# A block-sparse attention followed by a Fourier mix and an MLP: the planner that orders its instructions tries some hundred orders with shifted priorities

## The chip, the core and the metric

The kernel runs on one core of a Trainium2 chip. The metric is the device time of one execution in microseconds. Before the change the median of three executions is 297.0 us (296.93 to 297.16). One further execution was profiled; it took 297.32 us, of which the profile's span covers 295.1 us.

## The reference, cut to what matters

There are 4 batches of 8 heads, 768 positions and a head width of 64. For every query the mean key of each of 12 blocks of 64 keys is scored, the three best blocks and the query's own block are kept, and an ordinary causal softmax attention runs over the kept keys. Its output, laid out as `x` with 512 columns per position, is mixed by a two-dimensional Fourier transform and goes through an MLP:

```python
scores = np.where(mask & causal, scale * q @ k.T, -1e9)
x = softmax(scores) @ v                                  # per head, then heads side by side
mixed = np.real(np.fft.fft(np.fft.fft(x, axis=1), axis=2))
u = x + mixed
un = (u - mean(u)) / sqrt(var(u) + 1e-6)
out = u + np.maximum(un @ w_ch1, 0.0) @ w_ch2            # 512 -> 2048 -> 512
```

## The kernel before

**The work.** Two heads make a pair, and there are 16 pairs, four to a batch. `attention(p)` (line 455) loads q, k and v of a pair, casts them to 16 bits, turns k and q with TensorE (`k_turn` 496, `q_turn` 552; from the eighth pair on q is turned by a DMA on SP's queue), forms the block means (`k_sums` 509, `spread` 532), scores the blocks (`gates` 563), picks the best three (lines 588 to 626), turns the choice into a mask (`m_turn` 631, `spell` 638), and then runs, for each head, six chunks of scores (`scores` 657, matmuls on lines 661 and 666), each followed by an exponential on ScalarE (line 677), and one product with the values (`attend` 692, 21 matmuls on line 695) whose result VectorE divides by the row sums (lines 704 and 707). `fourier(b)` (718) needs the four pairs of its batch: VectorE or GpSimd forms sums and differences (lines 727 to 748), TensorE does the first transform (`stage1` 762, matmuls on lines 766 and 770) and the second (`stage2` 793, matmuls on line 800), VectorE adds x (806), takes statistics (813, 816), ScalarE makes the reciprocal deviation (824, 828), VectorE forms the bias (832), and `apply` (838, matmul input written on line 840 or 844) normalises. The first half of batch 0 is then turned by TensorE (`un_turn` 862, matmuls on line 864), everything else by a DMA on SP's queue (line 856). `mlp(b)` (956) runs 32 groups of four 384-column matmuls up (line 968), a clipping copy on ScalarE or VectorE (980, 982), and 24 groups of four 512-column matmuls down (line 997); the last batch's downward product is done with seven smaller products per block (`down_seven` 919, line 942).

**What sets the order.** None of this is issued as it is written. Every step is recorded by `Plan.op` (106) as an operation with a rank, the engines that could run it with a cost in us for each, the keys that it reads and writes, the PSUM banks that it uses, and for some a release time `rel`, before which the plan does not start it. `Plan.schedule` (139) then simulates five engines: again and again it takes, over all engines, the operation that could start first, with the lower rank going first between equals, and gives it to the engine on which it would end first. What comes out is one order for each engine's queue, and for operations that two engines could run, the engine. Only that order reaches the chip: each engine runs its list in order and waits on semaphores for its inputs, and neither the planned times nor the release times are kept there. Release times are given to the loads and casts of pairs 7 and later (`release`, 259: 70 us for pair 7, then 15.5 us a pair) and to the weights' DMAs on GpSimd's queue (`weight`, 390; first use in lines 1022 and 1026). The plan adds 0.5 us to what TensorE waits for from other engines after 70 us of plan time, and 2.5 us to what a DMA brings after the first 8 us.

**Fillers.** One thing of the plan other than the order does reach the chip. Until 75 us of plan time, where TensorE would sit idle for over 0.25 us ahead of an operation, the plan puts `int(idle / 0.2 + 1)` matmuls of 512 columns on a tile of zeros ahead of it (`filler`, 408, line 410); they write a spare bank that nothing reads. Eleven more stand at the very start. They are ordinary instructions in TensorE's queue: once issued they take their time whether or not the wait is there.

**Tiles in the profile.** `loads`, `turned`, `keys` and `vals` hold the attention's inputs, `x` its output, `fs` and `pm` the Fourier sums, `ty` and `tr` the half-transformed data, `u` the sum to be normalised, `unT` the turned normalised rows, `hT` the hidden layer, `w` the weights, `bank` any PSUM bank, `warm` the zeros of the fillers.

Of the kernel before, what the change touches and what calls it, by code (L numbers as in the profile page):

```python
# [2 lines left out]

# [78 lines left out]
class Plan:  # L83
# [22 lines left out]
    def op(self, rank, engs, fn, r=(), w=(), ps=(), dma=0.0, port=False, pre=(), after=(), rel=0.0,  # L106
# [29 lines left out]
        self.ops.append(o)  # L136
        return o

    def schedule(self):
        ops = self.ops  # L140
        free = dict(PE=1.0, ACT=1.5, DVE=0.9, POOL=1.3, SP=0.75)
        ready = {e: [] for e in free}
        for o in ops:
            o.wait = len(o.deps)
            o.ready = o.rel
            for d in o.deps:
                ops[d].users.append(o.i)
        cand = {e: set() for e in free}

        def offer(o):  # L150
            for e in o.engs:
                cand[e].add(o.i)

        for o in ops:
            if o.wait == 0:
                offer(o)
        banks = sorted((self.FILL_TO if b == self.SPARE else 0.0, b) for b in range(8))
        used = dict.fromkeys(self.CAPS, 0)
        releases = []
        dma_free = dict(POOL=0.0, SP=0.0)  # L160
        landing = {e: [] for e in free}
        port_free, holder = 0.0, None
        order = []
        left = len(ops)

        def begin(o, e, t):
            if o.port and e in ("DVE", "POOL"):
                t = max(t, port_free + (self.LAT["DVE"] if e == "POOL" and holder else 0.0))
            return max(t, free[e])

        while left:
            best = None
            for e, c in cand.items():
                now = free[e]
                pick = None
                for i in c:
                    o = ops[i]
                    t = o.ready
                    new = [p for p in o.ps if p.bank is None]
                    if new:  # L180
                        if len(banks) < len(new) or any(
                                used[p.kind] + len(new) > self.CAPS[p.kind] for p in new):
                            continue
                        t = max(t, banks[len(new) - 1][0])
                    if (o.dma or o.turn) and e != "POOL" and len(landing[e]) >= self.DEPTH:
                        t = max(t, landing[e][-self.DEPTH])
                    st = begin(o, e, t)
                    if len(o.engs) > 1:
                        end = st + o.engs[e]
                        if any(begin(o, x, t) + y < end - 1e-9 for x, y in o.engs.items() if x != e):  # L190
                            continue
                    key = (st, o.rank, i)
                    if pick is None or key < pick[0]:
                        pick = (key, o)
                if pick and (best is None or pick[0][0] < best[0][0]):
                    best = (pick[0], e, pick[1])

            if releases and (best is None or releases[0][0] <= best[0][0]):
                t, b, kind = heapq.heappop(releases)
                used[kind] -= 1  # L200
                banks.append((t, b))
                banks.sort()
                continue
            assert best is not None, "no work can start"
            (st, _, _), e, o = best
            for c in cand.values():
                c.discard(o.i)
            for p in o.ps:
                if p.bank is None:
                    p.bank = banks.pop(0)[1]  # L210
                    used[p.kind] += 1
            if e == "PE" and st < self.FILL_TO:
                o.fill = int((st - free[e]) / 0.2 + 1.0) if st - free[e] > 0.25 else 0
            o.eng, o.start = e, st
            free[e] = st + o.engs[e]
            if o.port and e in ("DVE", "POOL"):
                port_free = free[e]
                if e == "POOL":
                    o.hold, holder = holder, None
                elif st < self.HOLD_TO:  # L220
                    holder = o
            o.done = free[e] + self.LAT[e]
            if o.dma:
                mine, other = ("POOL", "SP") if e == "POOL" else ("SP", "POOL")
                go = max(dma_free[mine], free[e])
                shared = max(0.0, dma_free[other] - go)
                dma_free[mine] = go + (2 * o.dma if 2 * o.dma <= shared else o.dma + shared / 2)
                o.done = dma_free[mine] + (2.6 if e == "POOL" else 1.9)
                landing[e].append(o.done)
            if o.turn:  # L230
                o.done = free[e] + 1.2
                landing[e].append(o.done)
            order.append(o)
            left -= 1
            for p in o.ps:
                p.left -= 1
                if p.left == 0:
                    heapq.heappush(releases, (o.done, p.bank, p.kind))
            for u in o.users:
                v = ops[u]  # L240
                v.wait -= 1
                at = o.done
                if e in v.engs and len(v.engs) == 1 and not o.dma and not o.turn:
                    at = free[e] + self.OWN[e]
                elif o.dma or o.turn:
                    at += self.LANDING if st > 8.0 else 0.0
                elif "PE" in v.engs and o.done > self.SLACK_FROM:
                    at += self.SLACK
                v.ready = max(v.ready, at)
                if v.wait == 0:  # L250
                    offer(v)
        order.sort(key=lambda o: (o.start, o.i))
        return order
# [3 lines left out]


def release(p):
    return 0.0 if p < 7 else 70.0 + 15.5 * (p - 7)  # L260

# [20 lines left out]
def kernel(  # L284
# [10 lines left out]
    B, H, _, D = q.shape  # L295
# [87 lines left out]
    P = Plan()  # L383
# [19 lines left out]
    for i in range(2):  # L403
        small(0.2 + i, "DVE", 0.06,
              lambda x, n, i=i: nc.vector.memset(ind32[64 * i:64 * i + 64, i:i + 1], 1.0),
              r=["ind32"], w=["ind32"])

    def filler(n):
        for _ in range(n):
            nc.tensor.matmul(bank32[P.SPARE], warm[:, 0:128], warm, start=True, stop=True)  # L410
# [18 lines left out]
    def load(p, rank, what, e, q_="SP"):  # L429
        b, hp = divmod(p, HP)  # L430
        i = slot(p)
        t, dst, src = dict(k=("kn", kn[i][:, :, e, :], k), q=("qn", qn[i][:, e], q),
                           v=("vn", vn[i][:, e], v))[what]
        dma(rank, q_, dst, src[b, 2 * hp + e].rearrange("(st p) d -> p st d", p=128),
            [(t, i, e)], 0.72 if p < 3 else 0.85, rel=0.0 if p < 7 else max(60.0, release(p) - 18.0))
# [598 lines left out]

    made = {}
    with tc.manual_schedule():
        for o in P.schedule():
            filler(o.fill)
            made[o.i] = o.fn(o.eng, o)
            if o.hold is not None:  # L1040
                tc.add_manual_dep(made[o.i].ins, made[o.hold.i].ins.name, mybir.DependencyInfo(
                    mybir.DependencyClass.Sync, mybir.DependencyReason.DATA), reason="port")
# [30 lines left out]
```

## Time and profile before

| what | before |
|---|---|
| median of three executions | 297.0 us |
| the profiled execution | 297.32 us |
| its span | 295.1 us |
| TensorE (PE) busy, share of the span | 98% |
| VectorE (DVE) busy | 72% |
| ScalarE (ACT) busy | 61% |
| GpSimd (POOL) busy | 42% |
| filler matmuls on line 410 | 67 of 3011 matmuls |

PE is TensorE's matmuls and PEld its weight loads, which run beside them. The ends of matmuls are modelled in the profile and reach into the next matmul, so the time that a row of matmuls really took is read from the chain of waits, which gives start and length of consecutive pieces, and not from their mean duration. In the view by windows each engine's entry is its busy time in the stretch in us, with the number of instructions in brackets, then the granted TensorE clock, the DMA share and GB/s. In the timeline a row gives start, length, engine, line, operation, tiles and count, and in square brackets the idle time of that engine before the row, with what ended it.

### The profile page before, as it was taken

The page shows a single profiled execution, that of the slowest core. Times are in us where ns is not written, and L with a number is a line of the kernel's source. Part 1 is how long each engine was busy: PE and PEld are TensorE (multiplying, and loading weights), DVE is VectorE, ACT ScalarE, POOL GpSimd, SP SyncE. Part 2 cuts the span into 40 slices and gives each one's busy share as a digit, 9 for nine tenths or more (in the row PEclk, how much of TensorE's full clock was granted, in tenths as well). Part 3 has the DMA queues.
Part 4 walks back from the last instruction along what each step waited for, and adds up shares of the span by engine and source line. Part 5 has one row for each costly group of instructions (what it writes and reads, how often), then busy time and mean ns, then how long its engine had stood idle before and what let it go on. Part 6 is the DMA issues. An engine that isn't in the chain of part 4 may idle for free.

```text
span 295.1 us, 8026 instructions
## 1 busy us (share of the span) xinstructions
PE 289.9 (98%) x3011; PEld 196.6 (67%) x3011; DVE 213.8 (72%) x716; ACT 180.9 (61%) x398; POOL 125.1 (42%) x248
## 2 busy tenths in 40 slices
PE   8999999999999999999999999999999999999995
PEld 3778786866646677567656686566655764566884
DVE  4899999897735689967564979937936694047885
ACT  3479988877804787367808687288743863477100
POOL 5558787564729155646656185456111000000000
PEclk9999999999999999999999999999999999999999
DMA  8999999998349706498824837733001005200132
GB/s 206 259 238 231 214 286 206 198 216 146 71 101 258 165 0 136 114 211 186 191 61 90 198 56 170 153 75 89 3 36 38 37 2 125 89 2 0 35 109 71
DMA packets 108773, 37.41 MB, mean 127 GB/s; under 512 B 101192, under 2 KB 104948, under 8 KB 108736
## 3 DMA queue, kind: packets, MB, share of 16 engines
q1 hardware_dynamic: 104272, 32.06, 47.4%
q0 software_dynamic: 3536, 4.56, 8.8%
q8 instruction: 23, 0.38, 0.5%
q10 hardware_dynamic: 928, 0.30, 0.4%
q14 instruction: 14, 0.11, 0.1%
HBM read 28.52 MB, written 6.29 MB: 118 GB/s over the span
## 4 chain that ended last, share of the span: by engine, by line
PE 95%; DVE 1%; ACT 1%; POOL 1%; issue 1%; ACTq 0%; POOLq 0%
PE bank L968 28%; PE bank L997 21%; PE bank L666 12%; PE bank L695 6%; PE bank L942 6%; PE bank L410 6%; PE bank L800 3%; PE bank L766 3%; PE bank L498 2%; PE bank L517 1%; PE bank L554 1%; PE bank L661 1%; PE bank L633 1%; ACT turned L677 1%; PE bank L569 1%; PE bank L770 1%
## 5 line engine op out<-in xcount | busy, mean ns | idle before, releaser
L677 ACT ACTIVATE turned<-bank 128x512 f16<-128x512 f32 x192 | 89.0, 583 | 22.4 <-PE bank L666 21.6
L968 PE MATMUL bank<-unT,w 128*128 128x384 f16 x512 | 90.3, 326 | 0.0
L980 ACT ACTIVATE hT<-bank 128x384 f16<-128x384 f32 x111 | 54.6, 498 | 28.4 <-PE bank L968 27.3
L968 PEld LDWEIGHTS <-w 128*128 128x128 f16 x512 | 48.3, 98 | 29.9
L997 PE MATMUL bank<-w,hT 128*128 128x512 f16 x288 | 67.4, 379 | 0.0
L666 PE MATMUL bank<-turned,keys 76*128 76x128 f16 (+3 forms) x384 | 50.1, 259 | 0.0
L997 PEld LDWEIGHTS <-hT 128*128 128x128 f16 x288 | 26.6, 97 | 27.3
L666 PEld LDWEIGHTS <-keys 76*128 76x128 f16 x384 | 29.4, 97 | 11.5 <-issue 0.2
L683 POOL TENSOR_SCALAR_AFFINE_SELECT turned<-turned 128x512 f16<-128x512 f16 (+1 forms) x44 | 22.2, 523 | 30.5 <-ACT turned L677 24.7
L695 PEld LDWEIGHTS <-turned 128*128 128x128 f16 x672 | 24.1, 97 | 4.6 <-ACT turned L677 0.7
L486 POOL TENSOR_TENSOR loads<-loads 128x384 f16<-128x384 f32 x25 | 22.9, 917 | 7.4 <-DVE fs L727 2.8
L695 PE MATMUL bank<-vals,turned 128*128 128x65 f16 x672 | 25.5, 193 | 0.1
L643 DVE TENSOR_SCALAR turned<-bank 12x384 f16<-12x384 f16 x64 | 20.6, 321 | 6.0 <-issue 2.7
L715 POOL CAST loads<-loads 128x384 f16<-128x384 f32 x24 | 12.2, 508 | 22.9 <-DVE pm L738 5.9
L481 POOL TENSOR_TENSOR turned<-loads,turned 128x320 f16<-128x320 f32 x26 | 20.7, 795 | 1.0 <-DVE fs L727 0.7
L410 PE MATMUL bank<-warm 128*128 128x512 f16 x67 | 19.7, 428 | 1.3 <-DVE warm L398 1.3
L704 DVE RECIPROCAL rcp<-bank 128x6 f32<-128x6 f32 x32 | 6.0, 189 | 19.1 <-PE bank L695 16.9
L1003 DVE TENSOR_TENSOR u<-bank,u 128x512 f32<-128x512 f32 x18 | 12.4, 687 | 8.7 <-PE bank L997 7.2
L707 DVE TENSOR_TENSOR x<-bank,rcp 128x384 f16<-128x384 f32 x32 | 17.7, 554 | 0.7
L714 ACT COPY keys<-bank 64x768 f16<-64x768 f16 x11 | 8.8, 797 | 14.9 <-PE bank L498 13.2
L806 DVE TENSOR_TENSOR u<-bank,x 128x512 f32<-128x512 f32 x24 | 15.4, 678 | 1.2 <-PE bank L800 1.2
L813 DVE BATCH_NORM_STATS2 bst<-u 128x6 f32<-128x512 f32 x24 | 15.6, 670 | 0.0
(112 smaller groups left out, 409.5 us busy)
## 6 DMA issues: line engine op xcount, KB each, us to landing
loads<-in_k_dram SPq DMA_DIRECT2D x28, 192.0 KB, 3.5
loads<-in_v_dram SPq DMA_DIRECT2D x28, 192.0 KB, 3.7
loads<-in_q_dram SPq DMA_DIRECT2D x26, 192.0 KB, 3.4
out_dram<-u SPq DMA_DIRECT2D x18, 256.0 KB, 2.3
w<-in_moe_w_ch_dram POOLq DMA_DIRECT2D x16, 256.0 KB, 7.2
out_dram<-u SPq DMA_DIRECT2D x12, 128.0 KB, 1.7
hT<-in_k_dram SPq DMA_DIRECT2D x4, 192.0 KB, 3.8
hT<-in_q_dram SPq DMA_DIRECT2D x4, 192.0 KB, 3.8
```

The costliest lines, as they stand in the source:

```text
L410: nc.tensor.matmul(bank32[P.SPARE], warm[:, 0:128], warm, start=True, stop=True)
L481: lambda x, n, hi=hi, lo=lo, e=e: eng[x].tensor_tensor(out=lo, in0=qn[a][:, e, 1:NST], in1=hi[:, 1:NST], op=OP.subtract),
L486: lambda x, n, kh=kh, kl=kl, e=e: eng[x].tensor_tensor(out=kl, in0=kn[a][:, :, e, :], in1=kh, op=OP.subtract),
L643: nc.vector.tensor_scalar(out=rows[:, i::2, :], in0=turned[at:at + NB, 0:3 - i, :], scalar1=-NEG, scalar2=NEG, op0=OP.mult, op1=OP.add)
L666: nc.tensor.matmul(bank32[sp.bank][:, co:co + a1 - a0], KI[e][g3][0:76, 128 * jt:128 * jt + 128], QG[e][g3][0:76, a0:a1], start=not added, ...
L677: lambda x, n, sp=sp, pt=pt, at=at, wid=wid: nc.scalar.activation(out=pt[:, at:at + wid], in_=bank32[sp.bank][:, 0:wid], func=AF.Exp, scal ...
L683: lambda x, n, pt=pt, at=at, nd=nd: nc.gpsimd.affine_select(out=pt[:, at:at + 128 * nd].rearrange("p (a c) -> p a c", a=nd), in_=pt[:, at: ...
L695: nc.tensor.matmul(o[:, st, 0:65], pt[:, col:col + 128], V16[v4][:, e, jt, 0:65], start=(i == 0), stop=(i == 20))
L942: nc.tensor.matmul(bank32[mp.bank][:, 0:256], A[i][:, z, :], Bm[i][:, z, :], start=(z == 0), stop=(z == 7))
L968: nc.tensor.matmul(bank32[hp_.bank][:, 0:384], w1[:, dt, 128 * it:128 * it + 128], unT[:, dt, 384 * hf:384 * hf + 384], start=(dt == 0), s ...
L980: nc.scalar.activation(out=o, in_=i_, func=AF.Relu)
L997: nc.tensor.matmul(bank32[cp.bank], hT[hf][:, it, 128 * j:128 * j + 128], w2[:, it, :], start=(it == 0), stop=(it == NIT - 1))
```

## The change

The plan is no longer made once. `Plan.search` makes it, then 600 times moves something at random, makes the plan again, and keeps the move if the planned end is no later. What it moves are the release times over 59 us (one of them and all later ones together, or one to three of them apart) and the ranks between 0 and 30000 (all ranks in a stretch of 8, 100 or 500 together, or one, two or four of them apart). The random numbers start from a fixed seed, so that the same order comes out on every build. The starting point differs in one number as well: the release of pairs 8 and later is spaced by 15.0 us and not by 15.5. `Plan.schedule` itself is rewritten to be quicker; it picks by the same rule. No operation, cost, tile or instruction of the computation is added or taken away. The number of fillers is part of what a plan decides.

```diff
+    def search(self, rounds, seed):
+        rng = random.Random(seed)
+        groups = {}
+        for o in self.ops:
+            if 0 < o.rank < 30000:
+                groups.setdefault(("rank", o.rank), []).append(o)
+            if o.rel > 59.0:
+                groups.setdefault(("rel", o.rel), []).append(o)
...
+        last = max(o.done for o in self.schedule())
+        for _ in range(rounds):
+            what = rng.random()
+            if what < 0.15:
+                at, by = rng.choice(rels), rng.gauss(0, rng.choice([0.5, 2, 5]))
+                moved = [(g, by) for g in rels if g >= at]
...
+            elif what < 0.75:
+                at, wide = rng.choice(ranks)[1], rng.choice([8, 100, 500])
+                by = rng.gauss(0, rng.choice([20, 200, 800]))
+                moved = [(g, by) for g in ranks if at <= g[1] < at + wide]
...
+            self.reset()
+            try:
+                end = max(o.done for o in self.schedule())
+            except AssertionError:
+                end = last + 1.0
+            if end <= last + 1e-9:
+                last = end
+            else:
+                for o, rank, rel in old:
+                    o.rank, o.rel = rank, rel
+        self.reset()
+        return self.schedule()
...
 def release(p):
-    return 0.0 if p < 7 else 70.0 + 15.5 * (p - 7)
+    return 0.0 if p < 7 else 70.0 + 15.0 * (p - 7)
...
-        for o in P.schedule():
+        for o in P.search(600, 7):
             filler(o.fill)
             made[o.i] = o.fn(o.eng, o)
```

More of the change, by code (lines that the diff above doesn't have):

```diff
@@ L2 @@
 import heapq
+import random
 from contextlib import ExitStack
@@ L137, in op, with reset @@
         return o
+    def reset(self):
+        for o in self.ops:
+            o.users = []
+            o.eng = o.start = o.done = o.hold = None
+            o.fill = 0
+            for p in o.ps:
+                p.left, p.bank = 0, None
+        for o in self.ops:
+            for p in o.ps:
+                p.left += 1
+    def search(self, rounds, seed):
+        rng = random.Random(seed)
+        groups = {}
+        for o in self.ops:
+            if 0 < o.rank < 30000:
+                groups.setdefault(("rank", o.rank), []).append(o)
+            if o.rel > 59.0:
+                groups.setdefault(("rel", o.rel), []).append(o)
+        rels = sorted(g for g in groups if g[0] == "rel")
+        ranks = sorted(g for g in groups if g[0] == "rank")
+        last = max(o.done for o in self.schedule())
[4 more added lines that the diff above has]
+                moved = [(g, by) for g in rels if g >= at]
+            elif what < 0.3:
+                moved = [(g, rng.gauss(0, rng.choice([0.3, 1, 3])))
+                         for g in rng.sample(rels, rng.choice([1, 2, 3]))]
+            elif what < 0.75:
[3 more added lines that the diff above has]
+            else:
+                moved = [(g, rng.gauss(0, rng.choice([5, 50, 500])))
+                         for g in rng.sample(ranks, rng.choice([1, 2, 4]))]
+            old = [(o, o.rank, o.rel) for g, _ in moved for o in groups[g]]
+            for (name, _), by in moved:
+                for o in groups[(name, _)]:
+                    setattr(o, name, getattr(o, name) + by)
+            self.reset()
[5 more added lines that the diff above has]
+                last = end
+            else:
+                for o, rank, rel in old:
+                    o.rank, o.rel = rank, rel
+        self.reset()
+        return self.schedule()
     def schedule(self):
@@ L172, in schedule @@
             best = None
-            for e, c in cand.items():
-                now = free[e]
+            for e in sorted(free, key=free.get):
+                c, now = cand[e], free[e]
+                if best is not None and now > best[0][0]:
+                    break
                 pick = None
+                limit = best[0][0] if best is not None else 1e9
                 for i in c:
@@ L178, in schedule @@
                     t = o.ready
-                    new = [p for p in o.ps if p.bank is None]
+                    if (t if t > now else now) > limit:
+                        continue
+                    new = [p for p in o.ps if p.bank is None] if o.ps else None
                     if new:
@@ L186, in schedule @@
                         t = max(t, landing[e][-self.DEPTH])
-                    st = begin(o, e, t)
+                    st = begin(o, e, t) if o.port else (t if t > now else now)
+                    key = (st, o.rank, i)
+                    if st > limit or pick is not None and key > pick[0]:
+                        continue
                     if len(o.engs) > 1:
[L189 to L194, printed above, removed]
+                        end = st + o.engs[e] - 1e-9
+                        for x, y in o.engs.items():
+                            if x != e and begin(o, x, t) + y < end:
+                                break
+                        else:
+                            pick, limit = (key, o), st
+                        continue
+                    pick, limit = (key, o), st
                 if pick and (best is None or pick[0][0] < best[0][0]):
```

## The prediction

> **What bounds the kernel now.** I read the page first, for which engine the time belongs to.
>
> ```profile
> span 295.1 us, 8026 instructions
> ...
> PE 289.9 (98%) x3011; PEld 196.6 (67%) x3011; DVE 213.8 (72%) x716; ACT 180.9 (61%) x398; POOL 125.1 (42%) x248
> ...
> DMA  8999999998349706498824837733001005200132
> ```
>
> TensorE is busy nearly throughout, but a busy matmul row need not be useful work. So I cut the span at three points of the chain of waits: 62.94, where the last big group of fillers begins; 66.63, where the first MLP matmul (L968) starts; and 273.62, where the last product (L942) starts.
>
> ```profile
> 0.00:62.94 62.94, 60.90 (x896) 45.85 (x897) 54.52 (x219) 47.77 (x106) 43.07 (x75) 1.00 1.08 229
> 62.94:66.63 3.69, 3.69 (x28) 2.04 (x27) 3.51 (x19) 2.10 (x3) 1.73 (x6) 1.00 1.23 205
> 66.63:273.62 206.99, 206.99 (x1924) 132.46 (x1923) 140.14 (x435) 130.54 (x288) 80.26 (x169) 1.00 0.44 100
> 273.62:292.00 18.38, 18.34 (x169) 16.20 (x166) 15.18 (x45) 0.49 (x1) 0.00 (x0) 1.00 0.22 72
> ```
>
> From 66.63 to 292.0 TensorE has no gap (the second number of a row is its busy time). The same view for the fillers' line alone (L410) shows where they stand, and the chain of waits gives the pace of equal matmuls at different places (start, length, count):
>
> ```profile
> 0.00:66.60 66.60, 19.63 (x67) 6.32 (x67) 1.00 1.09 228
> 66.60:295.10 228.50, 0.03 (x1) 0.00 (x0) 1.00 0.42 97
> ```
>
> ```profile
> 1.27 5.73 PE bank L410 x13
> ...
> 12.24 1.32 PE bank L410 x6
> ...
> 62.94 1.94 PE bank L410 x9
> ...
> 65.55 1.08 PE bank L410 x5
> ...
> 100.67 5.86 PE bank L968 x36
> ...
> 148.20 5.19 PE bank L997 x24
> ...
> 242.46 10.36 PE bank L997 x48
> 252.82 20.80 PE bank L968 x128
> ```
>
> L968 runs at 5.86/36 = 163 ns a matmul at 100 us, amid attention, and at 20.80/128 = 163 ns at 253 us, where nothing else is left; L997 at 216 ns at both places. So nothing is hidden under modelled ends: after 66.6 us TensorE does a fixed amount of useful work at its own pace, and the planner cannot shorten that, only break it. What it can shorten is the head. There, all 67 fillers stand. Thirteen take 5.73 us at the start, at 441 ns each; the other 54 run at 1.94/9 = 216 ns, and 54 x 0.216 = 11.7 us. Beside them the head holds little visible idle time: 62.94 - 60.90 = 2.04 us, of which 1.27 us is before the first filler. TensorE's own waits say the same:
>
> ```profile
> PE bank L410 <- DVE warm L398: 1.3, 1, 1.3
> PE bank L498 <- ACT turned L714: 0.4, 1, 0.4
> PE bank L534 <- DVE ka L527: 0.2, 1, 0.2
> ```
>
> So the kernel is bound by TensorE's queue, fillers included, and its only movable part is some 12 us of fillers ahead of 66.6 us.
>
> **The change part by part.** The instruction orders of the two built programs tell what the search did. TensorE has the same useful matmuls in both, and the same ones ahead of the first L968 group; its last 72 operations stand in the same order, and so do SP's last 14 DMAs, so the end after TensorE (292 to 295.1) stays. Line 410 has 58 matmuls instead of 67. Counted by place: the 13 at the start, 4, 2 and 2 more before 18 us, 3 near 33 us and the 5 just ahead of the first L968 group stay. Between 12 and 15 us, 6 + 3 + 3 become 5 + 3 + 2. Near 36 us, 5 become 4. Between 47 and 61 us, 3 + 4 + 2 + 3 become 6 + 2 + 3, in other places. Ahead of the first `un_turn` (L864), 9 become 4.
>
> *The nine fillers.* At 0.216 us each: two at 12 to 15 us, 0.43; one at 36 us, 0.22; one net at 47 to 61 us, 0.22; five ahead of L864, 1.08. Sum 1.94 us.
>
> *Is the wait behind them gone as well?* A filler taken out where its wait stays gives nothing, so I look at the largest place, which is the chain that leads to the MLP.
>
> ```profile
> 57.35 1.31 PE bank L800 x12
> ...
> 64.88 0.67 PE bank L864 x12
> ```
>
> ```profile
> 57.82 1.89 DVE L806 TENSOR_TENSOR u<-bank,x 128x512 f32<-128x512 f32 x3
> ...
> 62.53 0.68 DVE L806 TENSOR_TENSOR u<-bank,x 128x512 f32<-128x512 f32 x1
> 63.13 0.15 DVE L832 SCALAR_TENSOR_TENSOR nmr<-stat,rstd 128x3 f32<-128x3 f32 x1
> ...
> 64.00 0.53 DVE L844 TENSOR_SCALAR x<-u,stat,rstd 128x512 f16<-128x512 f32 x1
> ```
>
> ```profile
> 58.98 0.60 ACT L677 ACTIVATE turned<-bank 128x512 f16<-128x512 f32 x1 [0.76 <-PE bank L666]
> 59.84 2.23 ACT L677 ACTIVATE turned<-bank 128x512 f16<-128x512 f32 x5 [0.26 <-PE bank L666]
> 61.92 0.33 ACT L824 ACTIVATE lnv<-stat,eps 128x3 f32<-128x3 f32 x1
> ...
> 63.31 1.52 ACT L840 ACTIVATE x<-u,nmr,rstd 128x512 f16<-128x512 f32 x2 [0.82 <-DVE nmr L832]
> ```
>
> The first normalised tile leaves ACT near 63.31 + 0.76 = 64.07 (two in 1.52 us), and the third tile at 63.31 + 1.52 = 64.83; L864 follows at 64.88, the end of the nine fillers. So of the 1.08 us up to 0.8 is filler that overshoots the first tile. The rest needs the chain itself to be earlier. In the changed order it is. Between the last two `stage1` groups and the first L800 stood six chunks of scores, `spread` and three fillers; now four chunks stand there and no filler (3 x 0.216 = 0.65 us for the fillers alone), so L806 starts earlier. And the L666 chunks for which ACT idled 0.76 + 0.26 = 1.02 us ahead of L677 stand closer together, ahead of both products with the values, so L824, behind twelve exponentials in both orders, comes about 1 us earlier. What is late next is `unT`'s copy, under the five fillers that stay.
>
> *Waits that come back.* At the three smaller places (0.43 + 0.22 + 0.22 = 0.86 us) no row says whether the wait goes too. The bounds: all comes back, which leaves 1.08; or none does and the 0.77 us of visible idle time after the first filler goes as well, which makes 2.7. The fillers overshoot there too (a planned idle time is rounded up to whole fillers), so I stay close to the plan and take 0.15 us back.
>
> *Everything after 66.6 us.* Ranks and release times moved nearly everywhere, and 69 operations change engine (33 copies on L714/L715, 23 clipping copies, 8 normalisations, 4 Fourier sums, one difference). As long as every input is there in time this is worth 0: cover is TensorE's own queue, without a gap over 206.99 us. If the cover goes, each late input costs its lateness in full; that is rival B. Release times matter only as order: SP's loads of pairs 7 to 15 now stand in other places between the DMA transposes. The busy DMA share after 66.63 is 0.44, so transfers have room.
>
> *Sum.* 297.32 - 1.94 + 0.15 = 295.5 us on the profiled execution (span 293.3). That execution stands 0.32 us above the median of 297.0, so the median comes out at **295.2 us**.
>
> **The rivals.**
>
> A. *The waits take the fillers' place.* If the chain through DVE and ACT sets the first L968, the nine fillers are replaced by idle time: 297.0, give or take 0.3. For it: DVE is busy 54.52 of the first 62.94 us and 3.51 of the next 3.69. Against: L864 started when the fillers ended, and only 0.77 us of idle time is visible in front of 62.94.
>
> B. *ScalarE becomes the bound near 200 us; slower.* In the changed order the last product with the values stands ahead of 24 L997 groups and 51 L968 groups, before ahead of 14 and 48. That is 10 x 4 x 0.216 + 3 x 4 x 0.163 = 10.6 us earlier, so the exponentials of the last pairs have to be done that much sooner.
>
> ```profile
> 190.00:200.00 10.00, 10.00 (x114) 6.46 (x112) 5.17 (x22) 7.02 (x15) 5.40 (x15) 1.00 0.42 107
> 200.00:205.00 5.00, 5.00 (x50) 3.36 (x48) 2.95 (x9) 4.24 (x10) 3.74 (x6) 1.00 0.35 83
> 205.00:210.00 5.00, 5.00 (x62) 3.45 (x61) 4.94 (x12) 5.00 (x13) 0.64 (x1) 1.00 0.04 8
> ```
>
> ```profile
> L677 ACT ACTIVATE turned<-bank 128x512 f16<-128x512 f32 x192 | 89.0, 583 | 22.4 <-PE bank L666 21.6
> ```
>
> ACT (the fourth engine entry) has 2.98 + 0.76 + 0 = 3.7 us free there, six exponentials of 0.583 us. It decides from the seventh that has to be pulled forward: twelve, one pair's, would be 7.0 - 3.7 = 3.3 us late, and the time 295.2 + 3.3 = 298.5. Against: TensorE can place MLP groups between, and ACT's whole load from 66.63 to 273.62 is 130.54 of 206.99.
>
> C. *TensorE's clock falls.* The first 13 fillers took 441 ns each, later ones 216, while the granted clock reads 1.00 in both windows; so the array starts slow in a way that this column does not show, and fillers end that. If one of the thinned places let it fall again, the price is that of the start: 13 x (0.441 - 0.216) = 2.9 us, so 298.1. Against: the longest wait of TensorE after the start is 0.4 us, and the planner still fills every planned wait over 0.25 us in the head. The Trainium skill (TensorE: Matmul & The Clock Gate, "What's actually happening") has the rule for it: half rate after about 3.4 us of an idle window, full rate after as long a busy one. The start of this trace took longer, 5.73 us of busy fillers before the first fast row; no row here shows the fall.
>
> D. *More than fillers goes*: the other bound above, 297.0 - 2.7 = 294.3.
>
> That the search kept nothing is excluded by the orders: nine fillers are gone.
>
> **How the numbers follow.** Forecast 0.72 (295.2, between 294.6 and 296.1), D 0.10, A 0.08, B 0.07, C 0.03. Faster by over 0.2% (below 296.4, about what a measurement of this kernel can tell from no change) are the forecast and D, 0.82; the same is A, 0.08; slower are B and C, 0.10. The range goes from D's time to A's, 294.3 to 297.0; outside lie B, C and half of A and D, 0.19.
>
> **What would show it.** Right: 58 matmuls on L410; the first L968 near 64.8 instead of 66.63; from there to the end of L942 the same 225.4 us; ACT's two idle times ahead of L677 near 59 gone. Wrong: TensorE idle rows ahead of L864 or L800 (A); pieces of ACT L677 in the chain after 190 us, or busy TensorE time below the window's length there (B); L666 or L864 matmuls at twice their pace in the head (C). A first L968 as early as forecast with a time that is not would put the fault after 66.6 us.

## The result and the profile after

The changed kernel takes 295.74 us (median of five executions, 295.36 to 295.79) against 297.0 us for the kernel before in the same measurement (296.89 to 297.16): ratio 0.9952, 95% interval 0.9941 to 0.9962. So it is about 1.3 us faster, where 1.8 us were forecast. The profiled execution took 295.36 us, which is the fastest of the five, 0.38 us under their median; the profiled execution before stood 0.32 us above its own. So the two traces differ by more (1.96 us) than the medians do. In the changed kernel's file the lines of the code stand 66 further down: fillers are L476, the matmuls up L1034, the last product L1008, `un_turn` L930, `stage2` L866, the attention's scores L732, and the copies out of PSUM L780 (ScalarE) and L781 (VectorE).

The page of the changed kernel:

```profile
span 293.6 us, 8001 instructions
...
PE 287.7 (98%) x3002; PEld 194.6 (66%) x3002; DVE 210.5 (72%) x704; ACT 185.0 (63%) x407; POOL 129.2 (44%) x251
...
L476 PE MATMUL bank<-warm 128*128 128x512 f16 x58 | 16.3, 412 | 1.3 <-DVE warm L464 1.3
```

58 fillers, as the orders said. Now the span is split as before, at the start of the last fillers, of the first matmul up and of the last product, in the view by windows (length, then busy time of PE, PEld, DVE, ACT, POOL, granted clock, DMA share, GB/s), and the pieces of the chain of waits that give these points (start, length, count):

```profile
0.00:61.32 61.32, 59.27 (x892) 44.71 (x893) 53.82 (x217) 49.35 (x109) 43.51 (x74) 1.00 1.07 225
61.32:63.95 2.63, 2.63 (x23) 1.55 (x22) 2.63 (x8) 2.17 (x4) 0.81 (x1) 1.00 1.19 200
63.95:271.90 207.95, 207.42 (x1924) 132.15 (x1923) 138.35 (x436) 133.03 (x294) 84.90 (x177) 1.00 0.50 103
271.90:290.25 18.35, 18.35 (x169) 16.20 (x166) 15.26 (x45) 0.49 (x1) 0.00 (x0) 1.00 0.22 72
```

```profile
61.32 0.88 PE bank L476 x4
62.20 0.67 PE bank L930 x12
62.87 1.08 PE bank L476 x5
63.95 4.55 PE bank L1034 x28
...
251.11 20.80 PE bank L1034 x128
271.91 18.35 PE bank L1008 x168
```

The head, which is all that stands ahead of the first matmul up, ends 2.68 us earlier (63.95 instead of 66.63), more than the nine fillers. But the stretch behind it, with the same 1924 matmuls, is 207.95 us long and not 206.99: 0.96 us of the gain is given back. TensorE is no longer busy throughout there, and all its visible idle time lies in one place. The row of the four us from 106, first for the kernel before and then for the changed one:

```profile
106.00:110.00 4.00, 4.00 (x47) 3.57 (x45) 2.59 (x7) 3.22 (x7) 3.06 (x9) 1.00 0.00 0
```

```profile
106.00:110.00 4.00, 3.47 (x31) 2.24 (x29) 2.34 (x6) 3.34 (x9) 0.05 (x1) 1.00 0.03 6
```

0.53 us of visible idle time is the whole difference of 207.95 and 207.42. More hides under modelled ends, as the timeline of TensorE there shows (start, length, engine, line, tiles, count, in brackets the idle time before):

```profile
107.17 0.38 PE L732 MATMUL bank<-turned,keys 76*128 76x128 f16 x4 [0.18 <-DVE tr L781]
107.39 0.20 PE L600 MATMUL bank<-ka,sm 128*128 128x24 f16 x2
107.45 0.81 PE L1034 MATMUL bank<-unT,w 128*128 128x384 f16 x4
108.27 0.75 PE L866 MATMUL bank<-cds,ty 128*128 128x256 f16 x4
109.36 1.03 PE L866 MATMUL bank<-cds,ty 128*128 128x256 f16 x8 [0.34 <-DVE tr L781]
```

Four L866 take 0.75 us here, while eight take 1.03; the pause between the fourth and the fifth is longer than the 0.34 us that show. What TensorE waits for is the end of VectorE's copies to `tr`. `ty` and `tr` are the second Fourier step's input of batch 1, and two engines copy them out of PSUM. The matmuls that wait do not read `tr` (their rows have `ty`, and the scores on L732 have neither). In the plan they write the bank that the copy before them reads: the second group of L866 gets the bank of `stage1`'s fourth result, and the scores get that of its second. So they wait for a bank to come free. The two engines' timelines, ScalarE first:

```profile
105.45 1.05 ACT L780 CAST ty<-bank 128x386 f16<-128x386 f32 x2 [0.60 <-DVE tr L781]
...
107.62 1.06 ACT L780 CAST ty<-bank 128x386 f16<-128x386 f32 x2 [0.66 <-DVE tr L781]
```

```profile
104.83 0.58 DVE L781 CAST tr<-bank 128x384 f16<-128x384 f32 x1
106.53 1.05 DVE L781 CAST tr<-bank 128x384 f16<-128x384 f32 x2 [1.12 <-ACT ty L780]
108.72 0.59 DVE L781 CAST tr<-bank 128x384 f16<-128x384 f32 x1 [1.13 <-ACT ty L780]
```

Read together: VectorE copies, then ScalarE, then VectorE, and none of them starts before the other has ended, from 104.83 to 109.31. Each of `stage1`'s four results lies in one PSUM bank and is copied twice, as `ty` and, with its columns reversed, as `tr`. Here ScalarE makes the one and VectorE the other, and each engine's copy waits for the other's from the same bank. The plan has no rule for this: `Plan.op` knows which step writes a bank and who reads it, and holds two reads free of each other; the plan starts the two copies of each of the four banks within 0.04 us of each other. The Trainium skill (PSUM — Partial Sum Buffer, "PSUM bank collisions raise a hardware error") says that the compiler's back end adds a dependency between two instructions of different engines on the same bank and the same quarter (32 partitions) of it, ScalarE against VectorE too; the waits of 1.12 and 1.13 us are in agreement with it.

The kernel before has the same wait at the same step, in VectorE's timeline:

```profile
107.70 1.09 DVE L715 CAST tr<-bank 128x384 f16<-128x384 f32 x2 [1.00 <-ACT ty L714]
...
109.20 1.10 DVE L715 CAST tr<-bank 128x384 f16<-128x384 f32 x2 [0.41 <-ACT ty L714]
```

There it cost nothing, because two groups of MLP matmuls stood between the two steps: the last of these copies ended at 110.30, and the first L800 came only at 110.88. The theory that the experiments test: the new order has put the second step so close behind the first that this wait, which the plan doesn't know, lands on TensorE.

### The profile page after: what moved, and what is told of

It is laid out like the page before. It is cut to its first block, busy times and chain, and to the rows that moved or that the text cites. A ratio compares the mean times of both kernels' runs of the same rounds, so it can differ in the third digit from the quotient of the medians.

```text
span 293.6 us, 8001 instructions
## 1 busy us (share of the span) xinstructions
PE 287.7 (98%) x3002; PEld 194.6 (66%) x3002; DVE 210.5 (72%) x704; ACT 185.0 (63%) x407; POOL 129.2 (44%) x251
## 4 chain that ended last, share of the span: by engine, by line
PE 89%; DVE 5%; ACT 2%; DMA 2%; issue 1%; POOL 0%; DVEq 0%; POOLq 0%
PE bank L1034 26%; PE bank L1063 21%; PE bank L732 12%; PE bank L761 7%; PE bank L1008 6%; PE bank L866 4%; PE bank L476 3%; DMA loads<-in_q_dram 2%; PE bank L564 1%; PE bank L620 1%; PE bank L832 1%; PE bank L583 1%; ACT ty L780 1%; PE bank L727 1%; DVE tr L781 1%
## 5 line engine op out<-in xcount | busy, mean ns | idle before, releaser
L743 ACT ACTIVATE turned<-bank 128x512 f16<-128x512 f32 (+1 forms) x192 | 89.7, 601 | 12.5 <-PE bank L732 12.1
L1034 PE MATMUL bank<-unT,w 128*128 128x384 f16 x512 | 90.7, 326 | 0.0
L1046 ACT ACTIVATE hT<-bank 128x384 f16<-128x384 f32 x114 | 56.7, 501 | 37.5 <-PE bank L1034 36.8
L1034 PEld LDWEIGHTS <-w 128*128 128x128 f16 x512 | 48.4, 98 | 29.7
L732 PE MATMUL bank<-turned,keys 76*128 76x128 f16 (+3 forms) x384 | 51.2, 258 | 0.3 <-DVE tr L781 0.2
L732 PEld LDWEIGHTS <-keys 76*128 76x128 f16 x384 | 29.8, 97 | 12.8 <-issue 0.5
L547 POOL TENSOR_TENSOR turned<-loads,turned 128x320 f16<-128x320 f32 x25 | 19.8, 792 | 1.4 <-DVE fs L793 0.8
L780 ACT COPY keys<-bank 64x768 f16<-64x768 f16 x14 | 11.1, 794 | 11.1 <-PE bank L564 8.6
L476 PE MATMUL bank<-warm 128*128 128x512 f16 x58 | 16.3, 412 | 1.3 <-DVE warm L464 1.3
L781 POOL CAST loads<-loads 128x384 f16<-128x384 f32 x24 | 12.3, 514 | 11.4 <-issue 3.0
L1014 DVE TENSOR_TENSOR u<-u,bank 128x256 f32<-128x256 f32 x36 | 13.1, 415 | 3.1 <-PE bank L1008 2.2
```

Source lines behind the costliest of these rows:

```text
L547: lambda x, n, hi=hi, lo=lo, e=e: eng[x].tensor_tensor(out=lo, in0=qn[a][:, e, 1:NST], in1=hi[:, 1:NST], op=OP.subtract),
L732: nc.tensor.matmul(bank32[sp.bank][:, co:co + a1 - a0], KI[e][g3][0:76, 128 * jt:128 * jt + 128], QG[e][g3][0:76, a0:a1], start=not added, ...
L743: lambda x, n, sp=sp, pt=pt, at=at, wid=wid: nc.scalar.activation(out=pt[:, at:at + wid], in_=bank32[sp.bank][:, 0:wid], func=AF.Exp, scal ...
L1034: nc.tensor.matmul(bank32[hp_.bank][:, 0:384], w1[:, dt, 128 * it:128 * it + 128], unT[:, dt, 384 * hf:384 * hf + 384], start=(dt == 0), s ...
L1046: nc.scalar.activation(out=o, in_=i_, func=AF.Relu)
```

## The experiments

In all, the time is split as above with two points of the chain of waits: the start of the first matmul up, and the start of the last product. Heads of equal order (after, e1 and e2) still start the first matmul up 0.7 us apart; the chain of waits begins with the first loads there, and the same product, L620 after GpSimd's first work, starts at 9.95 us in one and at 10.55 in another. The stretch between shows no such spread: it is 207.95 to 207.97 us in after, e4 and e6, which share it, and 206.99 in before and in e3.

| kernel | median, us (range) | ratio to before [95%] | first up | last product | between |
|---|---|---|---|---|---|
| before | 297.0 | | 66.63 | 273.62 | 206.99 |
| after | 295.74 (295.36 to 295.79) | 0.9952 [0.9941, 0.9962] | 63.95 | 271.91 | 207.96 |
| e1 same engine | 294.44 (294.36 to 294.84) | 0.9910 [0.9897, 0.9924] | 64.56 | 271.38 | 206.82 |
| e2 exponential late | 296.87 (296.6 to 298.3) | 0.9995 [0.9984, 1.0006] | 64.63 | 273.52 | 208.89 |
| e3 before, trimmed | 296.48 (296.35 to 296.61) | 0.9975 [0.9966, 0.9985] | 65.84 | 272.83 | 206.99 |
| e4 after, padded | 297.66 (297.28 to 297.93) | 1.0014 [1.0005, 1.0023] | 66.27 | 274.24 | 207.97 |
| e5 spacing only | 298.23 (298.11 to 298.31) | 1.0039 [1.0026, 1.0051] | 66.43 | 274.49 | 208.06 |
| e6 fewer fillers | 294.89 (294.77 to 294.93) | 0.9926 [0.9914, 0.9937] | 63.52 | 271.47 | 207.95 |
| e7 no fillers | 298.25 (296.82 to 298.96) | 1.0034 [1.0022, 1.0047] | 66.41 | 274.53 | 208.12 |
| e8 seed 8 | 294.57 (294.31 to 295.21) | 0.9918 [0.9906, 0.9931] | 64.35 | 271.21 | 206.86 |
| e9 rule, seed 7 | 295.17 (294.91 to 296.23) | 0.9937 [0.9924, 0.9951] | 64.64 | 271.32 | 206.68 |
| e10 rule, seed 9 | 294.78 (294.61 to 295.34) | 0.9922 [0.9910, 0.9934] | 64.64 | 271.16 | 206.52 |
| e11 rule, seed 9, fewer | 293.34 (293.13 to 293.5) | 0.9870 [0.9857, 0.9883] | 63.12 | 269.71 | 206.59 |
| e12 same engine, fewer | 293.89 (293.54 to 294.21) | 0.9889 [0.9876, 0.9901] | 63.27 | 270.09 | 206.82 |

The median of the kernel before was 297.1 or 297.2 in the measurements of the experiments, so differences between medians below are good to some 0.2 us.

One part of the time lies in neither column: from the start of the last product to the end of the profiled execution, device time and not span. It is 297.32 - 273.62 = 23.70 us in the kernel before, 23.66 and 23.72 in e3 and e5, which make their plan once, 23.43 to 23.49 in every kernel searched without the later rule, and 23.59 to 23.83 with it (e9 to e11). So the searched order gains some 0.25 us more there, although it ends with the same last product. Within it, the time outside the profiled span is some 2.2 us in every execution of the kernel before and some 1.7 in every one of the changed kernel, while the span's own end grows by some 0.2 (295.1 - 273.62 = 21.48 to 293.6 - 271.91 = 21.69). No run shows the cause.

**e1: each bank's two copies on one engine.** Only the eight copies of batch 1 change engine, so that no bank is read by both.

```diff
+            if o.i in (911, 912, 914, 915, 917, 918, 920, 921):
+                o.eng = "ACT" if o.i in (911, 912, 917, 918) else "DVE"
```

> The changed order, with one edit: in the second batch's Fourier step both copies out of one bank (L780/L781) are on the same engine, two banks on ACT and two on DVE, at the same places of the order. Theory (the compiled program lets two engines copy out of one bank only one after the other, the plan does not know it, and TensorE pays at the first L866 near 108 us): the 0.3 + 0.2 + 0.7 us of TensorE stalls between 106 and 109.1 us go, and the time falls by 0.9 to 1.2 us from 295.7, to about 294.7. Rival (ACT is late because exponentials stand between the copies): the stalls stay, since ACT still has the same four copies and the same exponentials; 295.7.

Measured: 1.3 us faster than after, and the stretch is back at 206.82 us. TensorE's timeline and its window in this kernel:

```profile
107.73 0.81 PE L1034 MATMUL bank<-unT,w 128*128 128x384 f16 x4
108.37 1.47 PE L866 MATMUL bank<-cds,ty 128*128 128x256 f16 x12
```

```profile
106.00:110.00 4.00, 4.00 (x51) 3.42 (x49) 3.24 (x8) 3.42 (x8) 1.18 (x3) 1.00 0.12 28
```

All twelve L866 follow without a gap; in the changed kernel the last eight began only at 109.36. The exponential between ScalarE's copies is still there (106.21 in ScalarE's timeline). The wait between the two engines is the cause of the loss after the head.

**e2: the rival that an exponential delays the copies.** In the changed order an exponential (operation 797) sits between ScalarE's two pairs of copies. It is moved behind the last of them.

```diff
+        late = next(o for o in order if o.i == 797)
+        order.remove(late)
+        order.insert(1 + next(n for n, o in enumerate(order) if o.i == 920), late)
```

> The changed order, with one edit: the exponential that ACT runs between the copies of the second batch's Fourier step (106.05 to 106.65) stands behind the last of ACT's copies there. Theory (waits between the two engines on one bank): ACT sits waiting for DVE in that place anyway, so nothing changes; 295.7. Rival (ACT's own load): ACT's later two copies come about 0.45 us sooner and the time falls by as much; 295.3.

Measured: 1.1 us slower than after. ScalarE's timeline shows that the copies come no sooner, since they go on waiting for VectorE (108.31 here against 107.62, with a head that is 0.68 us longer); TensorE's shows what the edit broke:

```profile
108.31 1.05 ACT L780 CAST ty<-bank 128x386 f16<-128x386 f32 x2 [1.12 <-DVE tr L781]
```

```profile
109.87 0.81 PE L1034 MATMUL bank<-unT,w 128*128 128x384 f16 x4 [1.58 <-ACT turned L743]
```

The late exponential holds a PSUM bank that the next group of matmuls up has to have, 1.58 us. The rival falls with the first row. Neither expectation was met: a step moved back on ScalarE's queue also moves the moment its bank comes free, which I had not counted.

**e3: the old order with nine fillers fewer.** The counts are those that the search took out, in the kernel before.

```diff
+            o.fill -= {117: 1, 119: 1, 317: 1, 470: 1, 498: 5}.get(o.i, 0)
```

> The order of before, with nine fillers taken out near the places where the search took them: five ahead of the first L864, one each at four other groups. Theory (the new order shortens the chain under the fillers): only the overshoot goes, up to 0.8 us ahead of L864 and a little elsewhere, 296.0 to 296.5, and TensorE shows idle time ahead of L864. Rival (fillers alone, the order does nothing): minus 9 x 0.216 = 1.94, 295.1.

Measured: 0.6 us faster than before. The chain of waits and TensorE's waits:

```profile
62.80 0.82 ACT x L840
...
63.66 0.40 PE bank L864 x4
...
64.77 1.08 PE bank L410 x5
65.84 1.30 PE bank L968 x8
```

```profile
PE bank L864 <- ACT x L840: 0.5, 1, 0.5
```

L864 now waits for the normalised tile. So of 1.94 us of fillers the old order gives back two thirds as waits; for that part the new order was needed. The stretch, 206.99, is that of before.

**e4: the new order with nine fillers more.**

```diff
+            o.fill += {113: 1, 58: 1, 317: 1, 490: 1, 498: 5}.get(o.i, 0)
```

> The changed order, with nine fillers put back: five ahead of the first un_turn, one each at four other groups. Theory (TensorE's queue sets the head, fillers cost their own time): plus 9 x 0.216 = 1.94, so 297.6, and the loss near 108 us stays; slower than before, since the order alone then only has that loss. Rival (the gain came from the order, fillers lie in waits): under 1 us is lost, 296.0 to 296.5.

Measured: 1.92 us slower than after between the medians, where 9 x 0.216 = 1.94; 1.81 if each is first set against the kernel before of its own measurement. A closer comparison is with e1, whose order of the head is the same and whose L620 starts at 10.55, as here at 10.53: the first matmul up comes at 66.27 against 64.56, 1.71 us, which is eight fillers. The ninth, at 36 us, covers a wait that e1 and the changed kernel show at 39 us and this one does not:

```profile
PE bank L699 <- DVE gmp L692: 0.2, 1, 0.2
```

So in the new order eight of the nine fillers are paid in full and one lies over a wait.

**e5: the other starting number alone.** The new spacing of the releases, and one plan without a search; 67 fillers.

```diff
-        for o in P.search(600, 7):
+        for o in P.schedule():
```

> One part of the change alone: the quicker planner with the release spacing of 15.0 us, planned once, no search. It has the fillers of before, 67. Theory (the time follows the fillers in the head and stalls after it): the head stays as before, the later casts and loads only move in the order; 297.0, at most 0.4 more from a stall in a Fourier step. Rival (the spacing is part of the gain): 296 or less.

Measured: 1.1 us slower than before, more than expected. The head is that of before (66.43), the stretch 1.07 us longer. VectorE's timeline shows the same wait, this time in batch 2's Fourier transform, and TensorE's shows where it stands idle:

```profile
168.29 1.06 DVE L781 CAST tr<-bank 128x384 f16<-128x384 f32 x2 [1.13 <-ACT ty L780]
```

```profile
176.16 0.60 PE L732 MATMUL bank<-turned,keys 76*128 76x128 f16 x4 [0.36 <-DVE turned L709]
...
176.96 0.38 PE L732 MATMUL bank<-turned,keys 76*128 76x512 f16 x1 [0.16 <-DVE u L872]
```

These are two places, eight us apart. The chain of waits leaves TensorE at 170.03, runs through VectorE's and ScalarE's work on `u`, its statistics and `turned`, and comes back at 176.96; the copy to `tr` is not a piece of it. The kernel before has such a wait at the same step, 1.25 us, and no loss. So this loss is not shown to come from the bank: the wait may have had a part in making VectorE late, and no run tried it. What is shown: the new number alone gains nothing, so the gain needs the search. A search from the old number was not run.

**e6, e7: are the remaining fillers needed?** One filler less in every group (44 left; the edit below), and none but the eleven at the start (`o.fill = 0`).

```diff
+        order = P.search(600, 7)
+        for o in order:
+            o.fill = max(o.fill - 1, 0)
```

> The changed order, with one filler less in each of the 14 groups (44 on L476 instead of 58). Theory (a planned wait is rounded up to whole fillers, and the overshoot delays TensorE): 14 x 0.216 = 3.0 us of fillers go, some of it comes back as waits; the first L1034 comes 1 to 2 us sooner, and the time is 294.0 to 294.7. Rival (the fillers only fill waits): within 0.3 of 295.7. Rival clock: matmuls of the head run at half pace somewhere, and the time is over 295.7.

> The changed order without the 47 fillers of the plan (the eleven at the start stay). Theory (the wait behind the fillers is then set by DVE and ACT): the first L1034 comes 2 to 2.5 us sooner than with them and the time is 293.3 to 294.0, if TensorE keeps its pace. Rival clock: waits of 0.4 to 1.5 us now stand bare in the head; if the array slows, its matmuls there take twice as long (128-column ones 0.11 instead of 0.055 us each), and the time is 296 or more.

Measured: e6 is 0.85 us faster than after: 14 x 0.216 = 3.0 us of fillers went, and some 70% came back as waits. e7 is 2.5 us slower than after, and the view by windows shows one reason (the eighth entry is the granted clock):

```profile
8.00:10.00 2.00, 1.44 (x21) 0.98 (x18) 1.93 (x7) 0.80 (x1) 1.11 (x2) 1.00 1.29 254
10.00:12.00 2.00, 1.41 (x40) 1.33 (x41) 1.76 (x4) 1.67 (x4) 1.49 (x3) 1.00 1.17 256
12.00:14.00 2.00, 0.93 (x13) 0.71 (x12) 1.48 (x15) 1.71 (x4) 1.36 (x2) 0.85 1.32 233
14.00:16.00 2.00, 2.00 (x32) 1.60 (x30) 1.73 (x6) 0.76 (x2) 0.00 (x0) 0.50 1.14 209
...
22.00:24.00 2.00, 2.00 (x23) 1.58 (x21) 1.16 (x3) 0.77 (x2) 2.00 (x4) 0.59 1.22 275
24.00:26.00 2.00, 2.00 (x42) 1.67 (x40) 1.84 (x6) 1.81 (x4) 0.75 (x2) 1.00 1.18 267
```

```profile
15.72 1.81 PE bank L732 x8
```

From 8 to 14 us TensorE is busy for 3.78 of 6 us; then the granted clock is 0.50 for some eight us. Eight L732 take 1.81 us there and 0.93 in the kernel before (L666) and the changed one. That is rival C's mechanism, and it is real: fillers are not only padding. It needs far more of them gone than the search took: with 41 left (e11) TensorE is busy for 5.54 of the same 6 us, and the clock reads 1.00. How much of the 2.5 us is the clock and how much bare waits was not separated. In three of the twelve executions, among the slowest (298.74 to 298.96), the mean clock reads 1.00; they have no trace, and the column did not show the slow start of the kernel before either.

**e8: another seed.**

```diff
-        for o in P.search(600, 7):
+        for o in P.search(600, 8):
```

> The change with another seed of the search (8 instead of 7): another order, of almost the same planned length, with 59 matmuls on L476. Theory (what the plan does not know, the copies of one bank by two engines, costs by chance in the changed order): the loss near 108 us is not there or elsewhere and smaller, and the time is 294.6 to 295.2. Rival (every searched order loses about 1 us after the head, since the search wears out all slack): 295.7 or more.

Measured: 1.2 us faster than after with one filler more (59). The head is ordinary (64.35), and the stretch has no loss (206.86). So the loss near 108 us belongs to one order; a searched order need not have it.

**e9, e10: the plan learns the rule.** A step of another engine may read a bank only after the first has ended.

```diff
+        self.by, self.till = None, 0.0
...
+                    for p in o.ps:
+                        if e != "PE" and p.by not in (None, e):
+                            t = max(t, p.till)
...
+            if e != "PE":
+                for p in o.ps:
+                    p.by, p.till = e, free[e] + 0.05
```

> The change with one rule more in the plan: a second engine may copy out of a bank only after the first has ended. Same seed; the order differs, 58 matmuls on L476. Theory (that rule is what the plan lacked): no TensorE stall ahead of L866 after the head, DVE and ACT wait less for each other's copies, and the time is 294.4 to 295.0. Rival (the loss near 108 us came from worn-out slack in general): about 1 us is lost in some other place and the time stays at 295.7.

> The same rule with another seed (9), which ends with 55 matmuls on L476, three less than the change. Theory: no stall after the head, three fillers less are 0.65 us; 293.6 to 294.4. Rival: 295 or more.

Measured: both a little above what was expected. The stretch is short (206.68 and 206.52, and 206.59 in e11, which has e10's order). Of that 0.17 us is no gain: three matmuls (L706, `m_turn`) have moved from the stretch to the head, so that like for like it is 206.85 and 206.69. That is e1's length without e1's edit, so the rule does what it should. In e9 VectorE still waits for ScalarE in that place (lines stand 7 further down here than in the changed kernel):

```profile
DVE tr L788 <- ACT ty L787: 2.7, 2, 1.8
```

but TensorE does not: the plan knows of it and has put other work between. What was missed in e10 is the head: three fillers less came back in part as a wait of 0.6 us for `ka`. What was missed in e9 is the end: 23.83 us from the start of the last product, against 23.46 in e1.

**e11, e12: both steps together.** e10 and e1, each with one filler less in every group (e6's edit).

> The order of the run before this one, with one filler less in each group. Theory (overshoot of rounded-up waits, as the same edit gave 0.85 us on the changed order): another 0.6 to 1.0 us, 293.0 to 293.6. Rival clock (one filler less lets the array slow): matmuls at half pace in the head, 294.5 or more.

> Both repairs on the changed order: the four pairs of copies near 106 us engine by engine, and one filler less in each group. Theory (two separate places on TensorE's queue, so the gains add): 295.74 - 1.30 - 0.85 = 293.6. Rival (the stall near 108 us takes up what the head gives): 294.4.

Measured: 293.34 and 293.89 us. e11 is the fastest kernel of this study, 3.9 us under the kernel before, ratio 0.9870 [0.9857, 0.9883], and its gain over e10, 1.44 us, is larger than expected; e12's over e1 is 0.55. The removed fillers and the removed wait nearly add: e12 is 1.85 us faster than after, where e1 and e6 alone give 1.30 and 0.85.

## Why the prediction was right, and where not

The sign held, and so did the mechanism in the head, fewer fillers in TensorE's queue; 295.74 lies between 294.6 and 296.1, the forecast's own range. Behind the head the mechanism did not hold. Point by point:

- **"54 x 0.216" and the nine fillers, 1.94 us.** Right in the main: e4 measures 1.71 to 1.92.
- **"Is the wait behind them gone as well?"** Right. In the old order it isn't (e3: 0.6 us of gain, with a wait of 0.5 us for the tile of L840); in the new one it is, but for one filler of nine (e4). The predicted sign for it, ScalarE's two idle times ahead of its exponentials near 59 us, shows in ScalarE's timeline after: 0.54 us of them are left of 1.02, and the reciprocal deviation starts at 59.66 and not at 61.92; some 0.6 us of that is this execution's early head.

```profile
56.40 3.39 ACT L743 ACTIVATE turned<-bank 128x512 f16<-128x512 f32 x8 [0.54 <-PE bank L732]
59.66 0.30 ACT L890 ACTIVATE lnv<-stat,eps 128x3 f32<-128x3 f32 x1
```

- **"I take 0.15 us back."** Too small to check: visible idle time ahead of the last fillers is 61.32 - 59.27 = 2.05 us, against 2.04 before, but e4 shows one filler over a wait of 0.2 us. The head's surplus, 63.95 against the 64.8 that were forecast, is mostly that one execution: with the same order of the head e1 and e2 start at 64.56 and 64.63, that is 2.0 us ahead of before.
- **"Everything after 66.6 us ... As long as every input is there in time this is worth 0."** This step failed. The stretch became 0.96 us longer. The prediction gave the condition and the price ("each late input costs its lateness in full"), but looked for a late input at one place only, ScalarE's last exponentials near 200 us. That did not happen. What came late was the end of the copies to `tr` near 108 us, which hold the banks that TensorE writes next, and the row that told of it was in the trace of before: VectorE idle for 1.00 us, waiting for a copy by ScalarE from the same bank. It was free there, and so it was passed over. The step's other half, that the planner can only break this stretch and not shorten it, since "nothing is hidden under modelled ends", is off by less: with the same matmuls e1 and e10 (like for like) are 0.17 and 0.30 us under 206.99, so a little was hidden in the kernel before. The prediction had named the sign of such a fault itself: a first matmul up as early as forecast with a time that is not.
- **The end, taken as unchanged.** The sum carried the time outside the span over as it was. From the start of the last product on it became 0.25 us shorter (23.70 to 23.45), and the cause is open.
- **Rival A** (waits take the fillers' place) is what e3 is, in the old order. **Rival B** is right as a kind of loss, wrong in its place and size. **Rival C** is real, but only with nearly all fillers gone (e7). **D** (more goes than fillers) can't be told from the forecast: the head gave 2.0 us, where 1.79 were forecast and 2.7 was D's bound, and single heads spread by 0.7 us. The time itself was far from D's 294.3.

So the sum should have read -2.0 for the head, +0.96 for the stretch and -0.25 for the end, -1.3, beside -1.26 between the medians; it read -1.79, 0 and 0. That the time lies in the forecast's own range is in part luck: with the stretch's 0.96 alone the forecast of 295.2 would have become 296.2, just outside it, and the surpluses of the head and the end brought it back.

## What to carry to other kernels

When a planner reorders a kernel, look in the trace of before for waits that its plan doesn't know, also where they cost nothing now: they are free only as long as something stands between, and an order that is made shorter by the plan's own rules can take just that away (seed 7 did, seed 8 did not). Two ways mend it, to give both reads of a bank to one engine or to teach the plan the wait; here each brought the stretch back to a little less than it had been (206.82 us, and 206.69 to 206.85 like for like). Fillers that a plan sets from rounded-up idle times are work in the queue, and thinning them by one in each group paid (0.55 to 1.44 us) where removing them cost 2.5.

## What the runs showed of the hardware

- TensorE's clock fell without any long pause. In e7 the longest single wait of TensorE after the start, in the six us before the fall, was 0.75 us, and it was busy 63% of that time; then the granted clock read 0.50 for some eight us of full work, and 1.00 again by 24 us. The Trainium skill (TensorE: Matmul & The Clock Gate, "What's actually happening") tells of half rate after an idle window of about 3.4 us; here a window thinned by many short waits went ahead of it, and 5.54 us of work in the same six (e11) kept the clock at 1.00.
- ScalarE and VectorE, both only reading one PSUM bank, took turns: eight copies of some 0.55 us took 4.5 us on two engines (104.83 to 109.31). With a bank's copies on one engine they took 3.0 us (105.33 to 108.29 in e1's timelines).
